# Turning q and k of batch 2 by DMA instead of on the tensor engine, in a fused attention and feed-forward kernel

## The chip, the cores and the metric

The kernel runs on one core of a Trainium2 chip. The core has a tensor engine (PE, with a separate queue of weight loads, PEld), a vector engine (DVE), a scalar engine (ACT), GpSimd (POOL) and a sync engine (SP) that only issues transfers, and 16 DMA engines that serve them all. Each engine runs its own instructions strictly in the order in which the program gives them, and waits on semaphores for the others. The metric is device time in microseconds for one execution. Three runs of the kernel before took 352.36, 352.91 and 353.14 us, median 352.91.

## What is computed

Causal attention with a decay, for 8 batches, 8 heads, 576 positions and a head width of 64; its result, 4608 tokens of 512, goes through `x @ w_in`, `h - tanh(h)` and `@ w_out` with an inner width of 2048.

```python
scores = scale * np.matmul(q, k.transpose(0, 1, 3, 2))
cum = np.cumsum(np.log(np.clip(f, 0.0001, 1.0)), axis=-1)
scores = np.where(causal, -1000000000.0, scores + cum[:, :, :, None] - cum[:, :, None, :])
attn = softmax(scores)                       # over the last axis
x = (attn @ v).transpose(0, 2, 1, 3).reshape(B * S, H * D)
h = x @ w_in
out = (h - np.tanh(h)) @ w_out
```

## The kernel before, in words

The order of the work on all five engines is written out by hand. The outer loop runs over 32 *slots*, one for each pair of heads: slot p works on batch p // 4 and heads 2c and 2c+1 with c = p % 4. A slot has seven *tiles* (ti = 0 to 6), and each tile is one `scores` call: PE multiplies a strip of keys with queries into one of two PSUM banks (`ps_sc`), ACT takes the exponential (L324) into a buffer `e` (`el` for tile 3), and POOL masks the diagonal (L334). Tiles 0 to 2 belong to the first head, 4 to 6 to the second, 3 to both. At tile 2 of the next slot `values` multiplies the masked weights with v on PE (L346, one PSUM tile `av`, a single buffer), and DVE normalises the result (L353 to L355, `rs` and `xn`). `turn` then brings `xn` into a ring `XR` by a DMA transpose from SP (L369, L371).

Between the tiles the feed-forward work is dealt out as *items* of four or eight matmuls: `mlp1` (L397, `hps`, then tanh on ACT, L402, and a sum on DVE, L406) and `mlp2` (L432 for the first 512 tokens, L456 for the rest, which use Strassen's seven products; DVE makes the sums, L424, and the weight differences, L234). `TAKE` says how many items a slot gets: 2, 7, 6, 6, 6, 8, 8, 7, 7 in slots 4 to 12. When the slots are done the rest of the items runs alone. Item banks come from a ring (`RINGS`): three banks `ps_m` up to slot 10, and a fourth, `ps_tr`, from slot 11 (`widen(1)`).

Scores need q and k with the head width on partitions (`QT`, `KT`, each in two buffers by batch parity). There are two ways to that:

* Batches below `FAR` (0, 1 and 2): a whole tensor is loaded with `load_qk` (L90). For each pair, in the slot before it is needed, `trans` turns it by six PE transposes (L253) into PSUM (`ps_tr` from slot 4 on) and two copies bring the even and the odd columns to `QT` or `KT` (L266 on DVE, L264 on ACT). From slot 4 on, q's copies are one on DVE and one on ACT, k's are both on DVE. The turn of k stands at tile 2 ahead of `values`, that of q at tile 0.
* Later batches: `load_block` (L96) loads five blocks of rows from POOL's queue, `turn_block` (L101) turns each by a DMA transpose on SP's queue into `TQ` or `TK`, and `place` copies them to `QT` (L106 on ACT, L108 on DVE or POOL) and `KT`. There is one tile `TQ`.

A dictionary `LOADS`, keyed by (slot, tile), holds when each load, turn and copy is emitted; it comes right behind that tile's scores. POOL's loads use eight completion semaphores in turn, so that a load waits until the load eight before it has landed; that wait stands in POOL's own queue.

Of the kernel before, what the change touches and what calls it, by code (L numbers as in the profile page):

```python
# [17 lines left out]
FAR = 3  # L18
# [3 lines left out]
def kernel(  # L22
# [63 lines left out]
    TQ = qkp.tile([P, NPAIR, S], FP16, tag="TQ", name="TQ")  # L86
# [35 lines left out]
    lf = TQ[0:NH, :, :].rearrange("p c s -> p (c s)").bitcast(FP32)[:, 0:S]  # L122
# [35 lines left out]
    cum = TQ[0:NH, :, :].rearrange("p c s -> p (c s)").bitcast(FP32)[:, S:2 * S]  # L158
# [47 lines left out]
    LOADS.setdefault((NPAIR, 5), []).append(lambda: load_qk(qn, q, 2, 0, H))  # L206
    LOADS.setdefault((NPAIR, 6), []).append(lambda: load_qk(kn, k, 2, 0, H))
    for b in range(2, B):
        p0 = (b - 1) * NPAIR
        for n in range(NJ - 1):  # L210
            LOADS.setdefault((p0 + 1, n), []).append(lambda b=b, n=n: load_v_block(b, n, 0, H))
        LOADS.setdefault((p0 + 1, 4), []).append(lambda b=b: load_v_rest(b))
        LOADS.setdefault((p0, 0), []).append(lambda b=b: load_aug(b))
        if b < FAR:
            continue
        for n in range(NJ):
            qs, ts = ((p0 - 1, n), (p0, 4)) if b == FAR else ((p0 - 2, n + 2), (p0 - 1, 3 if b == FAR + 1 else 1))
            LOADS.setdefault(qs, []).append(lambda b=b, n=n: load_block(qb, q, b, n))
            LOADS.setdefault((p0, n), []).append(lambda b=b, n=n: load_block(kb, k, b, n))
            LOADS.setdefault(ts, []).append(lambda b=b, n=n: turn_block(TQ, qb, b, n))  # L220
            LOADS.setdefault((p0 + 1, 4), []).append(lambda b=b, n=n: turn_block(TK, kb, b, n))
        parts = [(dst, src, a, c) for dst, src in ((QT, TQ), (KT, TK)) for a in range(2) for c in (0, 2)]
        spots = [(p0, 3, "A"), (p0, 5, "A"), (p0 + 1, 0, "A"), (p0 + 1, 2, "A")] + [(p0 + 3, ti, "V") for ti in range(4)]
        if b == FAR:
            spots = [(p0 + 3, ti, eng) for ti, eng in zip((0, 1, 2, 0, 1, 2, 4, 5), "AVAPPPPP")]
        elif b == FAR + 1:
            spots[0:4] = (p0, 5, "A"), (p0, 6, "A"), (p0 + 1, 0, "A"), (p0 + 1, 2, "V")
        for (slot, ti, eng), (dst, src, a, c) in zip(spots, parts):
            LOADS.setdefault((slot, ti), []).append(lambda b=b, dst=dst, src=src, a=a, c=c, eng=eng: place(
                dst, src, b, a, c, eng))  # L230
# [5 lines left out]
    SPOTS = [(7, 1), (7, 2), (7, 4), (7, 5), (8, 1), (8, 2), (10, 6), (11, 0)]  # L236
# [6 lines left out]
    def trans(b, c, src, dst, early, copies, split=False):  # L243
# [25 lines left out]
        for fn in todo[:2]:  # L269
            fn()  # L270
        return todo[2:]

    def head_tiles(a):
        return [[(a, 0, 0, 512, 0)],
                [(a, 1, P, 448, 0), (a, 0, 512, 64, 448)],
                [(a, 2, 2 * P, 320, 0), (a, 3, 3 * P, 192, 320)]]

# [109 lines left out]
    def mlp1(u, ft, part=None):  # L387
        if part != 1:
            HP[(u, ft)] = bank("hps")
        hps = HP[(u, ft)]  # L390
        t0 = u * UW % RING
        parts = [(0, t0, min(UW, RING - t0))]
        if t0 + UW > RING:
            parts.append((RING - t0, 0, t0 + UW - RING))
        for o, t, n in parts:
            for ci in {None: range(NCH), 0: range(NCH - 1), 1: (NCH - 1,)}[part]:
                nc.tensor.matmul(out=hps[:, o:o + n], lhsT=win[:, ci, ft * P:(ft + 1) * P],  # L397
                                 rhs=XR[:, ci, t:t + n], start=(ci == 0), stop=(ci == NCH - 1))
        if part == 0:
            return  # L400
        th = tmp.tile([P, UW], FP32, tag="th", name="th")
        nc.scalar.activation(out=th, in_=hps, func=AF.Tanh, scale=-1.0)  # L402
        half, i, kt = ft // NK, ft % NK // 4, ft % 4
        if half == 0 and kt == 0:
            GQ[(u, i)] = gtp.tile([P, 2, NK // 2, UW], FP16, tag="gq", name="gq")
        nc.vector.tensor_tensor(out=GQ[(u, i)][:, half, kt, :], in0=hps, in1=th, op=ALU.add)  # L406
        if u >= PLAIN:
            at = (12, 13, 14, 15) if u == 1 else (3, 6, 9, 12)
            if ft in at:
                sums(u, "S3", at.index(ft))  # L410
# [100 lines left out]
    def start():  # L511
# [5 lines left out]
        k_rest = trans(*pairs[0], kn, KT, True, "VVVV", True)  # L517
        unread(22)
# [18 lines left out]
    def att_items(p):  # L537
# [7 lines left out]
        early = p < NPAIR  # L545
        for ti in range(len(TILES)):
# [7 lines left out]
            if p == 1 and ti == 3:  # L554
                put(last)
            for load in LOADS.get((p, ti), ()):
                items.append((load, False))
            at_q, at_k = (1, 3) if p == 0 else (0, 1) if early else (0, 2) if p == NPAIR else (0, 2)
            if ti == at_q and after and after[0] < FAR:
                put(trans, *after, qn, QT, early, "VV" if early else "VA")  # L560
# [32 lines left out]
    with tc.manual_schedule(engines=FIVE):  # L593
        bulk()
        for p in range(len(pairs) + 1):
# [3 lines left out]
            if p == 3 * NPAIR - 1:  # L599
# [48 lines left out]
```

## Time and profile before

| | us |
|---|---|
| median of three runs | 352.91 |
| the profiled execution, whole | 352.82 |
| its span, first to last instruction | 351.0 |
| PE busy | 336.5 |
| DVE busy | 259.9 |
| ACT busy | 236.0 |
| POOL busy | 167.6 |

The granted clock of the tensor engine is full in every slice. The start of `values` marks the slots: 31.08 us in slot 4, 44.26 in slot 5, 54.65 in slot 6, 63.05, 71.12, 80.27, 90.83 and 100.48 in slots 7 to 11, 110.17 in slot 12. The profiled execution lies within 0.1 us of the median, and outside the span 1.8 us are left. In a timeline a row gives start, duration, engine, line, operation, tiles, form and count of a run of equal instructions, and in brackets how long the engine had been idle and what ended that. The end of a matmul is modelled and includes the way through the array, so a stall of PE is read from start to start: a 512-column matmul follows the one before after 0.216 us.

### The profile page before, as it was taken

How to read it: one execution, taken by the hardware profiler on the slowest of the kernel's cores; microseconds unless marked ns; L12 is line 12 of the kernel's file. 1: busy time of each engine (PE TensorE's matmuls, PEld its weight loads, DVE VectorE, ACT ScalarE, POOL GpSimd, SP SyncE). 2: the span in 40 equal slices, each digit the busy share in tenths (PEclk: the TensorE clock that was granted, in tenths of full speed). 3: DMA queues.
4: the chain of work that ended last, by engine and by line, in shares of the span. 5: the costliest groups of instructions: out<-in, count | busy, mean ns of one | idle time of the engine just before them, and what ended most of it. 6: DMA issues, size and time to landing. Idle time of an engine off the chain costs nothing.

```text
span 351.0 us, 8590 instructions
## 1 busy us (share of the span) xinstructions
PE 336.5 (96%) x3253; PEld 230.7 (66%) x3253; DVE 259.9 (74%) x493; ACT 236.0 (67%) x433; POOL 167.6 (48%) x324
## 2 busy tenths in 40 slices
PE   8998888999889999999999999999999999999996
PEld 7476444555458655875588888855885587477485
DVE  7597577747799588767876787678767866876874
ACT  5587777668695778588868886888648841742640
POOL 8873563776499656575657564752322210000000
PEclk9999999999999999999999999999999999999999
DMA  9999999999978999699969996992031013003003
GB/s 112 144 166 202 192 206 127 112 150 175 113 62 110 152 169 133 77 172 159 114 78 179 151 111 88 174 157 42 23 102 49 18 36 122 0 2 120 0 6 115
DMA packets 144876, 38.79 MB, mean 111 GB/s; under 512 B 128148, under 2 KB 143236, under 8 KB 144836
## 3 DMA queue, kind: packets, MB, share of 16 engines
q0 software_dynamic: 92480, 18.39, 69.7%
q1 hardware_dynamic: 52356, 19.88, 29.7%
q8 instruction: 25, 0.41, 0.5%
q14 instruction: 15, 0.12, 0.1%
HBM read 36.85 MB, written 9.44 MB: 132 GB/s over the span
## 4 chain that ended last, share of the span: by engine, by line
PE 77%; DVE 11%; ACT 7%; issue 2%; DMA 1%; POOL 1%; ACTq 0%; DVEq 0%; POOLq 0%
PE hps L397 28%; PE ops L456 26%; PE ps L315 10%; PE av L346 6%; PE ops L432 3%; ACT e L324 3%; DVE KT L266 3%; DVE gq L406 2%; ACT th L402 2%; DVE QT L266 2%; DVE xn L355 1%; ACT QT L264 1%; PE t L253 1%; DVE gq L424 1%; DMA TQ<-in_f_dram 1%
## 5 line engine op out<-in xcount | busy, mean ns | idle before, releaser
L397 PE MATMUL hps<-XR,win 128*128 128x512 f16 (+1 forms) x640 | 141.4, 357 | 3.1 <-DVE gq L406 1.6
L406 DVE TENSOR_TENSOR gq<-hps,th 128x512 f16<-128x512 f32 x144 | 98.6, 687 | 33.1 <-ACT th L402 31.8
L324 ACT ACTIVATE e<-ps 128x512 f16<-128x512 f32 x192 | 110.0, 598 | 15.5 <-PE ps L315 7.9
L402 ACT ACTIVATE th<-hps 128x512 f32<-128x512 f32 x144 | 86.8, 604 | 49.5 <-PE hps L397 44.3
L334 POOL TENSOR_SCALAR_AFFINE_SELECT e<-e 128x128 f16<-128x128 f16 x168 | 60.6, 363 | 76.7 <-ACT e L324 74.8
L397 PEld LDWEIGHTS <-win 128*128 128x128 f16 x640 | 57.6, 97 | 50.3 <-issue 2.8
L315 PE MATMUL ps<-QT,KT 67*128 67x64 f16 (+5 forms) x384 | 77.2, 276 | 3.1 <-ACT e L324 2.4
L456 PEld LDWEIGHTS <-gq 128*128 128x128 f16 x640 | 60.3, 97 | 12.3 <-DVE gq L424 1.4
L456 PE MATMUL ops<-wout,gq 128*128 128x256 f16 x512 | 63.3, 272 | 1.1 <-DVE gq L424 1.1
L315 PEld LDWEIGHTS <-KT 67*128 67x128 f16 (+1 forms) x384 | 36.9, 98 | 27.9 <-issue 4.8
L346 PEld LDWEIGHTS <-e 128*128 128x128 f16 x896 | 32.1, 97 | 3.1
L346 PE MATMUL av<-vn,e 128*128 128x65 f16 x896 | 33.6, 193 | 0.0
L119 POOL DMA_DIRECT2D vn<-in_v_dram x32 | 28.0, 877 | 10.6 <-DMA win<-in_moe_w_in_dram 4.1
L456 PE MATMUL ops<-W,sq 128*128 128x256 f16 x256 | 31.2, 272 | 0.0
L355 DVE TENSOR_TENSOR xn<-av,rs 128x640 f16<-128x640 f32 x32 | 26.4, 825 | 1.1
L456 PEld LDWEIGHTS <-sq 128*128 128x128 f16 x256 | 24.2, 98 | 3.4
L266 DVE COPY KT<-t 64x576 f16<-64x576 f16 (+1 forms) x26 | 19.5, 750 | 3.8 <-PE t L253 3.6
L334 POOL TENSOR_SCALAR_AFFINE_SELECT el<-el 128x128 f16<-128x128 f16 x28 | 9.5, 338 | 26.8 <-ACT el L324 26.7
L96 POOL DMA_DIRECT2D qn<-in_q_dram x25 | 21.2, 846 | 0.7 <-issue 0.4
L96 POOL DMA_DIRECT2D kn<-in_k_dram x25 | 21.1, 846 | 0.6 <-issue 0.3
L106 ACT ACTIVATE QT<-TQ 64x1152 f16<-64x1152 f16 x17 | 19.7, 1158 | 0.2
L266 DVE COPY QT<-t 64x576 f16<-64x576 f16 x15 | 11.9, 795 | 7.6 <-PE t L253 7.6
(83 smaller groups left out, 301.9 us busy)
## 6 DMA issues: line engine op xcount, KB each, us to landing
out_dram<-ost SPq DMA_DIRECT2D x34, 256.0 KB
vn<-in_v_dram POOLq DMA_DIRECT2D x24, 128.0 KB, 5.6
qn<-in_q_dram POOLq DMA_DIRECT2D x20, 128.0 KB, 4.9
kn<-in_k_dram POOLq DMA_DIRECT2D x20, 128.0 KB, 4.5
win<-in_moe_w_in_dram POOLq DMA_DIRECT2D x2, 1024.0 KB, 14.8
wout<-in_moe_w_out_dram POOLq DMA_DIRECT2D x2, 1024.0 KB, 14.0
XR<-xn SPq DMA_TRANSPOSE x56
vn<-in_v_dram POOLq DMA_DIRECT2D x12, 64.0 KB, 4.8
```

What stands on the lines that cost most here:

```text
L96: nc.gpsimd.dma_start(out=dst[b % 2][0:pn, n, :].rearrange("p (h d) -> p h d", h=H), in_=src[b, :, n * P:n * P + pn, :].rearrange("h p d - ...
L119: nc.gpsimd.dma_start(out=vn[b % 2][:, n, h0:h1, 0:D], in_=v[b, h0:h1, n * P:(n + 1) * P, :].rearrange("h p d -> p h d"))
L266: nc.vector.tensor_copy(out=to, in_=of)
L315: nc.tensor.matmul(out=ps[:, col:col + n], lhsT=KT[b % 2][0:rows, h, j * P:(j + 1) * P], rhs=QT[b % 2][0:rows, h, i0:i0 + n], start=not ow ...
L324: nc.scalar.activation(out=e[:, lo:hi], in_=ps[:, lo:hi], func=AF.Exp, scale=qscale)
L334: nc.gpsimd.affine_select(out=view, in_=view, compare_op=ALU.is_ge, fill=0.0, base=0, pattern=pat, channel_multiplier=-1)
L346: nc.tensor.matmul(out=av[:, a, ib, :], lhsT=E.pop((b, c, a, j, ib)), rhs=vn[b % 2][:, j, 2 * c + a, 0:D + 1], start=(j == 0), stop=(j == ib))
L355: nc.vector.tensor_tensor(out=xn.rearrange("p i (a d) -> p a i d", a=2), in0=av[:, :, :, 0:D], in1=rs.to_broadcast([P, 2, NJ, D]), op=ALU. ...
L397: nc.tensor.matmul(out=hps[:, o:o + n], lhsT=win[:, ci, ft * P:(ft + 1) * P], rhs=XR[:, ci, t:t + n], start=(ci == 0), stop=(ci == NCH - 1))
L402: nc.scalar.activation(out=th, in_=hps, func=AF.Tanh, scale=-1.0)
L406: nc.vector.tensor_tensor(out=GQ[(u, i)][:, half, kt, :], in0=hps, in1=th, op=ALU.add)
L456: nc.tensor.matmul(out=ps[:, m, :], lhsT=LHS[lhs](u, kt // 4)[:, kt % 4, m * P:(m + 1) * P], rhs=rhs[:, kt, :], start=(fresh and (apart or ...
```

## The change

* `FAR` is 2: batch 2 goes the second way too. Its five blocks of q are loaded from tile 3 of slot 4 to tile 0 of slot 5, those of k in tiles 1 to 5 of slot 5, v in slot 6 instead of slot 5. q is turned on SP at (5, 2), k at (6, 1). ACT places q at (6, 5), (7, 0), (8, 1), (8, 5), DVE places k at (7, 2), (7, 4), (8, 2), (8, 6). The PE transposes of slots 7 to 10 and their copies are gone.
* `TQ` has two tiles, by batch parity.
* Of the remaining turns from slot 4 on (batch 1, slots 4 to 6) both q copies are on DVE, and of q and k the second copy is emitted a tile later (`LATER`, `rest`). In slots 5 and 6 the turn of k moves from tile 2, ahead of `values`, to tile 3, behind it.
* Batch 3: q is placed by ACT alone and k by DVE alone (before: ACT, DVE, ACT and five copies on POOL), in slots 11 and 12. Batch 4: all four q copies on ACT (before: three and one on DVE). For all later batches k's copies are spread over two slots, (p0+3, 0), (p0+3, 2), (p0+4, 1), (p0+4, 4).
* The four-bank ring starts at slot 7 instead of 11.
* The weight differences move to (7,1), (7,3), (7,5), (7,6), (8,0), (8,4), (9,5), (10,1), and the first Strassen sums `S3` of unit 1 come with `mlp1` steps 3, 6, 9, 12, as in the other units, instead of 12 to 15.

```diff
-FAR = 3
+FAR = 2
...
-    TQ = qkp.tile([P, NPAIR, S], FP16, tag="TQ", name="TQ")
+    TQ = [qkp.tile([P, NPAIR, S], FP16, tag=f"TQ{i}", name=f"TQ{i}") for i in range(2)]
...
-    LOADS.setdefault((NPAIR, 5), []).append(lambda: load_qk(qn, q, 2, 0, H))
-    LOADS.setdefault((NPAIR, 6), []).append(lambda: load_qk(kn, k, 2, 0, H))
...
     for b in range(2, B):
         p0 = (b - 1) * NPAIR
...
+        at_q = [(p0 - 2, n + 2) for n in range(NJ)]
+        at_k = [(p0, n) for n in range(NJ)]
+        at_v = [(p0 + 1, n) for n in range(NJ)]
+        to_q, to_k = (p0 - 1, 1), (p0 + 1, 4)
+        on_q = (p0, 3), (p0, 5), (p0 + 1, 0), (p0 + 1, 2)
+        on_k = (p0 + 3, 0), (p0 + 3, 2), (p0 + 4, 1), (p0 + 4, 4)
+        if b == 2:
+            at_q = [(p0, 3), (p0, 4), (p0, 5), (p0, 6), (p0 + 1, 0)]
+            at_k = [(p0 + 1, n + 1) for n in range(NJ)]
+            at_v = [(p0 + 2, n) for n in range(NJ)]
+            to_q, to_k = (p0 + 1, 2), (p0 + 2, 1)
+            on_q = (p0 + 2, 5), (p0 + 3, 0), (p0 + 4, 1), (p0 + 4, 5)
+            on_k = (p0 + 3, 2), (p0 + 3, 4), (p0 + 4, 2), (p0 + 4, 6)
+        elif b == 3:
+            at_q = [(p0 - 1, n) for n in range(NJ)]
+            to_q = p0, 4
+            on_q = (p0 + 3, 1), (p0 + 3, 3), (p0 + 3, 5), (p0 + 4, 1)
+            on_k = (p0 + 3, 2), (p0 + 3, 4), (p0 + 4, 0), (p0 + 4, 4)
...
+            add(to_q, turn_block, TQ[b % 2], qb, b, n)
+            add(to_k, turn_block, TK, kb, b, n)
+        for n, (c, a) in enumerate(((0, 0), (0, 1), (2, 0), (2, 1))):
+            add(on_q[n], place, QT, TQ[b % 2], b, a, c, "A")
+            add(on_k[n], place, KT, TK, b, a, c, "V")
...
-    SPOTS = [(7, 1), (7, 2), (7, 4), (7, 5), (8, 1), (8, 2), (10, 6), (11, 0)]
+    SPOTS = [(7, 1), (7, 3), (7, 5), (7, 6), (8, 0), (8, 4), (9, 5), (10, 1)]
...
-        for fn in todo[:2]:
+        n = 2 if early else 1
+        for fn in todo[:n]:
             fn()
-        return todo[2:]
+        LATER.extend(todo[n:])
+        return todo[n:]
...
+    def rest():
+        while LATER:
+            LATER.pop()()
...
-            at = (12, 13, 14, 15) if u == 1 else (3, 6, 9, 12)
+            at = 3, 6, 9, 12
...
+            if p >= NPAIR and ti in (at_q + 1, at_k + 1) and after and after[0] < FAR:
+                items.append((rest, False))
...
-            at_q, at_k = (1, 3) if p == 0 else (0, 1) if early else (0, 2) if p == NPAIR else (0, 2)
+        at_q, at_k = (1, 3) if p == 0 else (0, 1) if early else (0, 2) if p == NPAIR else (0, 3)
...
-                put(trans, *after, qn, QT, early, "VV" if early else "VA")
+                put(trans, *after, qn, QT, early, "VV")
...
-            if p == 3 * NPAIR - 1:
+            if p == 2 * NPAIR - 1:
                 widen(1)
```

More of the change, by code (lines that the diff above doesn't have):

```diff
@@ L120, in load_v_block @@
                             in_=v[b, h0:h1, n * P:(n + 1) * P, :].rearrange("h p d -> p h d"))
-    lf = TQ[0:NH, :, :].rearrange("p c s -> p (c s)").bitcast(FP32)[:, 0:S]
+    lf = TQ[0][0:NH, :, :].rearrange("p c s -> p (c s)").bitcast(FP32)[:, 0:S]
     nc.sync.dma_start(out=lf, in_=f.rearrange("b h s -> (b h) s"))
@@ L157 @@
     nc.scalar.activation(out=lf, in_=lf, func=AF.Ln)
-    cum = TQ[0:NH, :, :].rearrange("p c s -> p (c s)").bitcast(FP32)[:, S:2 * S]
+    cum = TQ[0][0:NH, :, :].rearrange("p c s -> p (c s)").bitcast(FP32)[:, S:2 * S]
     nc.vector.tensor_tensor_scan(out=cum, data0=ones16, data1=lf, initial=0.0,
@@ L205, with add @@
         LOADS.setdefault((3, n), []).append(lambda n=n: load_v_block(1, n, 2, H))
-    LOADS.setdefault((NPAIR, 5), []).append(lambda: load_qk(qn, q, 2, 0, H))
-    LOADS.setdefault((NPAIR, 6), []).append(lambda: load_qk(kn, k, 2, 0, H))
+    def add(where, fn, *args):
+        LOADS.setdefault(where, []).append(lambda: fn(*args))
     for b in range(2, B):
         p0 = (b - 1) * NPAIR
[L210 to L215, printed above, removed]
-        for n in range(NJ):
[L217 to L230, printed above, removed]
@@ new lines @@
+        add((p0, 0), load_aug, b)
+        for n in range(NJ):
+            add(at_q[n], load_block, qb, q, b, n)
+            add(at_k[n], load_block, kb, k, b, n)
+            if n < NJ - 1:
+                add(at_v[n], load_v_block, b, n, 0, H)
+            else:
+                add(at_v[n], load_v_rest, b)
+            add(to_q, turn_block, TQ[b % 2], qb, b, n)
[3 more added lines that the diff above has]
+            add(on_k[n], place, KT, TK, b, a, c, "V")
@@ L276, in head_tiles @@
                 [(a, 2, 2 * P, 320, 0), (a, 3, 3 * P, 192, 320)]]
+    LATER = []
+    def rest():
+        while LATER:
+            LATER.pop()()
     TILES = head_tiles(0) + [[(0, 4, 512, 64, 64), (1, 4, 512, 64, 128)]] + head_tiles(1)
@@ L517, in start @@
         k_rest = trans(*pairs[0], kn, KT, True, "VVVV", True)
+        LATER.clear()
         unread(22)
```

## The prediction, made before the changed kernel ran

> **What bounds the kernel now.** I read the page's busy times first, then PE's waits by stretch, then PE's timeline where a stall stands, then the other engines' timelines there.
>
> ```profile
> PE 336.5 (96%) x3253; PEld 230.7 (66%) x3253; DVE 259.9 (74%) x493; ACT 236.0 (67%) x433; POOL 167.6 (48%) x324
> ```
>
> PE leads. Its list of waits from 130 to 340 us is empty: from slot 14 on the time is PE's own work in sequence. So the change can win only before 130 us, in two ways: fewer PE instructions, or fewer stalls. PE's timeline:
>
> ```profile
> 41.37 1.03 PE L397 MATMUL hps<-XR,win 128*128 128x512 f16 x4
> 43.15 0.41 PE L253 MATMUL t<-id,kn 96*128 96x96 f16 x6 [0.75 <-ACT QT L264]
> 43.40 1.03 PE L397 MATMUL hps<-XR,win 128*128 128x512 f16 x4
> ...
> 54.40 0.42 PE L253 MATMUL t<-id,kn 96*128 96x96 f16 x6 [0.86 <-ACT QT L264]
> ...
> 88.67 0.38 PE L315 MATMUL ps<-QT,KT 67*128 67x320 f16 x2
> 89.71 0.41 PE L253 MATMUL t<-id,kn 96*128 96x96 f16 x6 [0.66 <-ACT QT L264]
> 89.97 1.03 PE L397 MATMUL hps<-XR,win 128*128 128x512 f16 x4
> ...
> 94.28 1.02 PE L397 MATMUL hps<-XR,win 128*128 128x512 f16 x4 [0.38 <-DVE gq L406]
> ...
> 105.32 0.39 PE L456 MATMUL ops<-wout,gq 128*128 128x256 f16 x2 [1.08 <-DVE gq L424]
> ```
>
> Two things are to be seen. Six transposes take 0.25 to 0.26 us from their start to the next row's (43.15 to 43.40). And a stall is larger than its bracket, because the end of a matmul is modelled late: four matmuls at 41.37 take 0.865, so PE stood from 42.24 to 43.15, 0.91 us. From start to start the stalls are: slots 4 to 6: 0.97 (before 33.38), 0.91, 0.80, 0.31, 1.02; slots 7 to 9: none; slots 10 and 11: 0.82, 0.54, 0.70 (before 96.06), 1.24; slots 12 to 14, all for exponentials of ACT: 0.39, 0.44, 0.53.
>
> **PE work removed.** 8 groups (slots 7 to 10, q and k) x 0.257 = 2.06 us, all on the path.
>
> **Stalls of slots 10 and 11.** The 0.82 is a turn of k waiting for ACT's copy out of the one bank of q's turn; it goes with the turn. The 0.54 and 0.70 wait for DVE to free one of three banks; slots 9 and 10 lose six DVE copies of 0.80 and get a fourth bank. The 1.24 waits for the last S3 sum: DVE runs without a gap from 97.75 to 106.4, and the change takes two weight differences (0.77 each), a q copy (0.65) and most sums out of that stretch. DVE in slot 10 then has 8 x 0.687 + 3 x 0.6 + 0.77 + 1.2 = 9.3 us against 8 items x 0.865 + 2.27 = 9.2 of PE, so it is level, with one bank more. I count 3.30 gone; bounds 2.0 and 3.3.
>
> **Stalls of slots 12 to 14.** Two stand behind three q copies of 1.16 us on ACT, one exponential between them (115.07, 116.62, 118.28); the third behind ACT's tanh waiting 0.87 for a DVE that had a q copy. The change spaces batch 4's copies as those of later batches stand, which stall nothing, but puts three more copies (3.5 us) on ACT in slots 11 to 13. ACT was busy 1.78 of 5 us from 110 to 115 and 2.78 from 120 to 125, so they fit. I take 0.9 of the 1.36; bounds: all gone, or 1.5 more.
>
> **Slots 4 to 6.** ACT's q copy goes to DVE, and with it ACT's wait for DVE's half (1.46 at 42.29); k's turn stands a tile later. Up to 4.0 us of stalls could go. But new waits follow, on transfers that PE's lead doesn't move:
>
> ```profile
> 31.11 0.82 POOL L119 DMA_DIRECT2D vn<-in_v_dram  x1 [4.12 <-DMA win<-in_moe_w_in_dram]
> 32.17 0.88 POOL L193 DMA_DIRECT2D wout<-in_moe_w_out_dram  x1
> 35.09 0.88 POOL L193 DMA_DIRECT2D wout<-in_moe_w_out_dram  x1
> ...
> 49.36 1.30 SPq L369 DMA_TRANSPOSE XR<-xn  x1
> ...
> 77.53 6.54 SPq L101 DMA_TRANSPOSE TQ<-qn  x5
> ...
> 42.29 0.81 ACT L264 ACTIVATE QT<-t 64x576 f16<-64x576 f16 x1 [1.46 <-DVE QT L266]
> ```
>
> (1) *POOL.* The first row shows POOL stopped 4.12 us for the landing of the load eight before. `wout` lands 12.9 and 15.2 us after issue, at 45.1 and 50.3. Ten block loads now follow it at once, and the third block of k, at (5, 3), is the eighth after the second `wout`: POOL stands from about 47 to 50.3. Behind it are the masks of tiles 4 to 6 of slot 5 and two loads of 0.88: 50.3 + 0.88 + 0.3 + 0.88 + 0.3 + 0.7 + 0.42 = 53.8. `values` in slot 6 needs them and ends about 54.3 (before: 55.55). Of 4.0 us only 1.25 are left.
>
> (2) *ACT behind TQ.* Loads of v of this shape landed 0.6 to 1.25 us apart, so q's blocks land from 51.2 to about 54.4. SP needs 1.3 each (6.54 for five): 51.3 to 57.8. Packets come later under bulk loads: the XR turn of 49.36 has none in its queue until 53.0. A quiet one lands about 2 us after issue. I take 60.5 for the last, bounds 59.2 and 63. ACT reaches (6, 5) at about 57.5 and blocks; the copy ends 61.65, the exponential of tile 6 at 62.2, and PE's (7, 1) scores, which need its bank and would start at 54.3 + 4 x 0.865 + 0.26 + 0.93 = 58.95, start at 62.25: a new stall of 3.3 us.
>
> (3) *DVE behind TK.* SP goes on with XR (2.6, to 60.4), then TK (6.5, to 66.9), landing 68.3. DVE's copy at (7, 2) waits for it, with rs, xn and the weight differences behind it; it ends 68.8. PE reaches slot 8 at 62.25 + 5 x 0.865 + 0.90 + 1.16 = 68.64, so it waits 0.15. `values` of slot 8 starts at 68.8 + 2 x 0.865 + 0.66 = 71.2, where before it started at 71.12, with four of the eight groups already gone. The xn of slot 7 comes at 70.0, that of slot 8 at 74.8; XR lands about 79.2 and `mlp1` of unit 1 asks at 80.4, so nothing is lost there.
>
> By start of `values` in slot 8, then, the change has lost 0.1 us, whatever was won in slots 4 to 6.
>
> The Trainium skill ("VectorE: DVE Perf Modes", The three transpose paths) gives 1309 ns for a DMA transpose of 128x128; one after another, the 18 squares of q would be 23.6 us by an estimate from it, TK would land past 98 us and the time would rise by about 27 us. The trace disagrees: five turns are issued in 6.54 us, and batch 3's TK, issued from 87.42, was read at 101.5.
>
> **Edits at nothing.** Two TQ tiles (SP waited 6.1 us for the one, with no PE wait behind it); k copies of later batches spread (0.46 each on a DVE with gaps; price 0 to 0.5); v in slot 6 (needed in slot 9, two slots after landing). Five copies of 1.1 to 1.6 us leave POOL in slot 11, hidden behind PE before.
>
> **Sum.** +0.1 (slots 4 to 8) - 1.03 (four groups of slots 9 and 10) - 3.30 - 0.9 = -5.1, from the profiled 352.8 (0.1 under the median): **347.7 us**.
>
> **The rivals.**
> *A, transfers later than that: slower.* Bulk loads starve SP's queue; every microsecond that TK lands after 68.3 delays slot 8 by as much. It decides from 68.3 + 5.1 = 73.4 us. For it: the turn of 49.36 took until after 57 in all. Against: later turns kept SP's pace beside loads. With TK at 75, 354.4. 0.14.
> *B, no new waits.* If the transfers hide, the front stalls stay away too: at the fastest SP issues, 1.2 each, TK lands near 67.2, which by (3) gives 1.1 more, and all of slots 12 to 14 gives 0.46: 346.1; without gates on transfers 342.7. 0.12.
> *C, ACT becomes the bound in slots 11 to 13.* Three more copies, 3.5 us, with only half hidden, and none of the 1.36 won: 347.7 + 0.9 + 1.8 = 350.4. For it: the stalls there were ACT's already. Against: the same spacing later. 0.12.
> *D, the clock.* A stall of 3.3 us is longer than any in the trace, whose longest is 1.24, and the clock was full throughout. If half the clock were granted for as long again, 3.3 us of work would take 6.6: 351.0. 0.05. The Trainium skill ("TensorE: Matmul & The Clock Gate", Why this matters for your kernels) warns of idle gaps over about 3 us between bursts, after which the clock halves; no run here shows it.
> *E, nothing happens.* What slots 10 and 11 stop losing is lost there to DVE, level with PE in slot 10, and only the groups remain: 347.7 + 3.3 + 0.9 + 0.8 = 352.7. 0.05.
>
> **How the numbers follow.** The forecast holds 0.52. The range takes in B's near end and C and D: 346.0 to 351.5, leaving out the most of A, E and the far end of B, 2 in 10. A change of 0.2%, 0.7 us, is about what can be told from none. Faster: forecast 0.52, B, C and D 0.29 = 0.81. Within 0.2%: 0.05, E. Slower: 0.14, A.
>
> **What would show it.** Right: no L253 after 60 us; the four stalls of slots 10 and 11 gone; a POOL load of k with an idle of some 3 us ended by `wout`; an ACT copy from TQ near 60 us with a wait before it; a PE stall of 2 to 4 us before scores of slot 7; `values` of slot 8 near 71. Wrong: DVE's copy from TK later than 73; PE stalls for exponentials in slots 11 to 13; a clock below full near 62 us.

## The result, and the profile after

The changed kernel takes 356.02 us (median; 355.24 to 357.21), the kernel before 352.55 beside it: a ratio of 1.0098, with an interval of 1.0073 to 1.0123. It is slower by 3.5 us, where 347.7 was forecast. The profiled execution took 355.64 us, so 7.9 us are to be explained.

The page of the changed kernel: its busy times, and the clock in 40 slices of 8.84 us.

```profile
PE 334.3 (95%) x3205; PEld 229.0 (65%) x3205; DVE 252.8 (72%) x490; ACT 239.7 (68%) x433; POOL 168.1 (48%) x327
...
PEclk9999999699999999999999999999999999999999
```

PE has 2.2 us less to do (334.3 for 336.5), and yet the span grew from 351.0 to 353.6. The clock, full throughout before, falls in one slice, from 62 to 71 us. Its list of waits (in total, times, longest):

```profile
PE ps L334 <- ACT e L343: 9.1, 10, 5.4
PE ps L334 <- DVE KT L277: 2.0, 2, 1.1
PE av L365 <- POOL e L353: 1.5, 2, 0.8
```

The waits for `gq` of slots 10 and 11 are gone; one wait of 5.4 us has come. PE's timeline shows where:

```profile
53.11 0.27 PE L365 MATMUL av<-vn,e 128*128 128x65 f16 x3 [0.69 <-POOL e L353]
...
54.16 0.45 PE L365 MATMUL av<-vn,e 128*128 128x65 f16 x9 [0.79 <-POOL e L353]
...
59.30 1.03 PE L451 MATMUL ops<-wout,gq 128*128 128x512 f16 x4
65.75 0.59 PE L334 MATMUL ps<-QT,KT 67*128 67x448 f16 x2 [5.43 <-ACT e L343]
66.15 1.90 PE L451 MATMUL ops<-wout,gq 128*128 128x512 f16 x4
...
73.75 0.60 PE L334 MATMUL ps<-QT,KT 67*128 67x320 f16 x3
...
111.37 0.38 PE L334 MATMUL ps<-QT,KT 67*128 67x448 f16 x2 [1.04 <-ACT e L343]
```

The four matmuls of 59.30 are through at 60.17 (4 x 0.216), so PE stood for 5.6 us. After it the same four take 1.90 instead of 1.03. The third matmul of the row at 73.75 is the first scores of slot 8, at 73.97. The other engines' timelines hold what PE waited for:

```profile
50.72 0.88 POOL L96 DMA_DIRECT2D kn<-in_k_dram  x1 [3.87 <-DMA wout<-in_moe_w_out_dram]
...
51.60 6.66 SPq L101 DMA_TRANSPOSE TQ<-qn  x5
...
60.96 8.10 SPq L101 DMA_TRANSPOSE TK<-kn  x5
...
64.06 1.16 ACT L106 ACTIVATE QT<-TQ 64x1152 f16<-64x1152 f16 x1 [5.77 <-DMA TQ<-qn]
...
72.44 0.63 DVE L108 COPY KT<-TK 64x1152 f16<-64x1152 f16 x1 [12.84 <-DMA TK<-kn]
```

ACT stood 5.77 us for TQ with the exponentials queued behind it, and DVE 12.84 us for TK. DVE's copy of TK was over at 73.07 (72.44 + 0.63), 0.9 us before PE came to the first scores of slot 8, so in this execution PE did not wait for TK there. And the clock, in stretches of 2 us (length; busy time and instructions of PE, PEld, DVE, ACT and POOL; the granted clock; the DMA engines' busy share; GB/s):

```profile
60.00:62.00 2.00, 0.33 (x2) 0.05 (x1) 0.00 (x0) 0.00 (x0) 0.01 (x1) 1.00 2.00 156
62.00:64.00 2.00, 0.00 (x0) 0.00 (x0) 0.00 (x0) 0.00 (x0) 0.00 (x0) 0.70 1.92 159
64.00:66.00 2.00, 0.25 (x1) 0.10 (x1) 0.00 (x0) 1.94 (x3) 0.23 (x1) 0.50 1.78 72
...
68.00:70.00 2.00, 2.00 (x34) 1.77 (x32) 0.00 (x0) 0.60 (x1) 1.81 (x4) 0.60 1.70 227
```

In stretches of 1 us the clock falls to one half at 62.8 and is full again at 69.6.

| start of values in slot | before | after | forecast |
|---|---|---|---|
| 5 | 44.26 | 41.54 | |
| 6 | 54.65 | 51.74 | |
| 7 | 63.05 | 68.27 | |
| 8 | 71.12 | 76.35 | 71.2 |
| 11 | 100.48 | 103.95 | |
| 14 | 129.35 | 131.58 | |
| end of span | 351.0 | 353.6 | |

The front won 2.9 us by slot 6 and lost 8.1 by slot 7. From slot 8 to the end 2.7 came back: 5.23 behind, then 2.53 (the spans are 353.58 and 351.05 before rounding). From the first scores of slot 8 to the end of the span the changed kernel takes 279.6 us.

### The profile page after: what moved, and what is told of

It is laid out like the page before. It is cut to its first block, busy times and chain, and to the rows that moved or that the text cites. A ratio compares the mean times of both kernels' runs of the same rounds, so it can differ in the third digit from the quotient of the medians.

```text
span 353.6 us, 8525 instructions
## 1 busy us (share of the span) xinstructions
PE 334.3 (95%) x3205; PEld 229.0 (65%) x3205; DVE 252.8 (72%) x490; ACT 239.7 (68%) x433; POOL 168.1 (48%) x327
## 4 chain that ended last, share of the span: by engine, by line
PE 83%; ACT 4%; DMA 3%; issue 3%; DVE 3%; SPq 1%; POOL 1%; ACTq 0%; POOLq 0%
PE hps L416 30%; PE ops L475 26%; PE ps L334 12%; PE av L365 8%; PE ops L451 3%; ACT e L343 3%; DMA TQ<-qn 2%; DMA kn<-in_k_dram 1%; DVE gq L425 1%; SPq L101 1%; PE ps L337 1%; PE t L264 1%; ACT th L421 1%; PE ps L305 1%; PE idle L524 1%
## 5 line engine op out<-in xcount | busy, mean ns | idle before, releaser
L353 POOL TENSOR_SCALAR_AFFINE_SELECT e<-e 128x128 f16<-128x128 f16 x168 | 60.4, 362 | 72.3 <-ACT e L343 70.2
L334 PE MATMUL ps<-QT,KT 67*128 67x64 f16 (+5 forms) x384 | 78.1, 278 | 11.3 <-ACT e L343 9.1
L475 PEld LDWEIGHTS <-gq 128*128 128x128 f16 x640 | 60.3, 97 | 11.0
L365 PEld LDWEIGHTS <-e 128*128 128x128 f16 x896 | 33.0, 98 | 5.3 <-POOL e L353 1.7
L365 PE MATMUL av<-vn,e 128*128 128x65 f16 x896 | 34.6, 194 | 1.5 <-POOL e L353 1.5
L106 ACT ACTIVATE QT<-TQ 64x1152 f16<-64x1152 f16 x24 | 27.9, 1163 | 6.3 <-DMA TQ<-qn 5.8
L96 POOL DMA_DIRECT2D kn<-in_k_dram x30 | 25.3, 845 | 6.3 <-DMA wout<-in_moe_w_out_dram 5.7
L96 POOL DMA_DIRECT2D qn<-in_q_dram x30 | 25.4, 846 | 3.0 <-issue 2.0
L108 DVE COPY KT<-TK 64x1152 f16<-64x1152 f16 x24 | 11.5, 481 | 13.2 <-DMA TK<-kn 12.8
L372 DVE TENSOR_SCALAR rs<-av 128x10 f32<-128x10 f32 x32 | 5.2, 162 | 21.8 <-PE av L365 21.7
```

Source lines behind the costliest of these rows:

```text
L96: nc.gpsimd.dma_start(out=dst[b % 2][0:pn, n, :].rearrange("p (h d) -> p h d", h=H), in_=src[b, :, n * P:n * P + pn, :].rearrange("h p d - ...
L106: nc.scalar.activation(out=to, in_=of, func=AF.Copy)
L334: nc.tensor.matmul(out=ps[:, col:col + n], lhsT=KT[b % 2][0:rows, h, j * P:(j + 1) * P], rhs=QT[b % 2][0:rows, h, i0:i0 + n], start=not ow ...
L353: nc.gpsimd.affine_select(out=view, in_=view, compare_op=ALU.is_ge, fill=0.0, base=0, pattern=pat, channel_multiplier=-1)
L365: nc.tensor.matmul(out=av[:, a, ib, :], lhsT=E.pop((b, c, a, j, ib)), rhs=vn[b % 2][:, j, 2 * c + a, 0:D + 1], start=(j == 0), stop=(j == ib))
L475: nc.tensor.matmul(out=ps[:, m, :], lhsT=LHS[lhs](u, kt // 4)[:, kt % 4, m * P:(m + 1) * P], rhs=rhs[:, kt, :], start=(fresh and (apart or ...
```

## The experiments

Each ratio is to the kernel before, run beside it (352.46 to 352.54 us median), with its interval. The theory after the result: batch 2's turned q and k arrive too late, TK above all, and slot 8 can't start before TK. The rivals: ACT's queue alone holds PE up, the clock costs on top, or other parts of the change cost it. "Too late" holds in what follows; "TK above all" does not: in which runs PE did wait for TK is said with each.

**q copied later** (e1_q_late).

```diff
-            on_q = (p0 + 2, 5), (p0 + 3, 0), (p0 + 4, 1), (p0 + 4, 5)
+            on_q = (p0 + 3, 4), (p0 + 3, 6), (p0 + 4, 1), (p0 + 4, 5)
```

> ACT's first two copies of batch 2's q move from (6, 5), (7, 0) to (7, 4), (7, 6), the last places that still lie before the scores of slot 8. Nothing else is changed. Theory 'transfers' (the landing of TK at 72.4 us sets the start of slot 8, whatever PE does before): the stall of 5.4 us before scores (7, 1) goes, but PE then reaches the scores of slot 8 near 66 us and waits there for DVE's copy of TK, to 73.1 us or later; values of slot 8 starts between 75 and 77, the time is 354.5 to 357. Rival 'ACT's queue' (the wait of ACT at (6, 5) alone holds PE up): the stall of 5.4 us and the slow clock of 3.3 us behind it go, no new stall comes: 347 to 348.5.

359.01 us, 1.0186 (1.0170 to 1.0201). The stall before (7, 1) is gone, and a larger one stands before the first scores of slot 8, in PE's timeline:

```profile
66.19 0.38 PE L334 MATMUL ps<-QT,KT 67*128 67x320 f16 x2
75.64 0.61 PE L334 MATMUL ps<-QT,KT 67*128 67x512 f16 x1 [9.06 <-DVE KT L108]
76.04 1.91 PE L451 MATMUL ops<-wout,gq 128*128 128x512 f16 x4
```

ACT's queue alone is not the cause: without its wait PE only came sooner to TK, and now it did wait for it. The time is worse than either theory had it, because TK was read at 75.13 us in this execution and the half clock (to 79.7) now fell wholly on work of slot 8.

**PE kept busy in the stall** (e2_warm).

```diff
+            if p == 7 and ti == 1:
+                items.append((lambda: unread(95), False))
```

> 95 matmuls of 128 columns on constants, into a bank that nobody reads, are put ahead of the scores (7, 1), where PE stands idle from 60.2 to 65.7 us. All waits stay. If an idle PE is what halves the clock, the clock stays full from 62 to 70 us. Theory 'the clock is hidden' (what PE loses at half clock it would have lost waiting for TK): scores (8, 0) move from 74.1 to about 73.2 us, 354.6 to 355.5. Rival 'the clock adds to the stall': 3.3 us less, 352.2 to 353.2. If the clock drops all the same, something else drops it, and the time stays at 356.

355.0 us, 1.0061 (1.0043 to 1.0079). PE's timeline and the stretch of the clock in this run:

```profile
70.71 0.39 PE L334 MATMUL ps<-QT,KT 67*128 67x512 f16 x1 [0.43 <-DVE KT L108]
```

```profile
64.00:66.00 2.00, 2.00 (x39) 1.48 (x38) 0.00 (x0) 1.91 (x3) 1.46 (x4) 1.00 1.26 145
```

An idle PE is what halved the clock: with matmuls in the gap it stays full. And PE now waits for TK at slot 8. In the changed kernel PE came to those scores 0.9 us after the copy of TK had ended; that is what the clock could cost there. The difference of the two ratios is 1.3 us, uncertain by 1.1 (both intervals together), so a cost of 0.9 fits. The 3.3 us of the rival were also my mis-sizing: from 65.75 to 69.6 at half clock 1.9 us are lost, and times alone don't tell 1.9 from 0.9; the wait for TK in the trace does.

**Without the loads of v of batch 2** (e3_no_v2).

```diff
-            if n < NJ - 1:
+            if b == 2:
+                pass
+            elif n < NJ - 1:
                 add(at_v[n], load_v_block, b, n, 0, H)
```

> The five loads of v of batch 2 in slot 6 are left out (batch 2 then works with batch 0's v, and its rows of the output are those of another v). The turns of q and k on SP's queue run beside these loads from 54 to 68 us. Theory 'the turns share the DMA engines with the loads of v': TQ lands near 61.5 instead of 64.0, TK near 69 instead of 72.4, the stall before (7, 1) shrinks to about 3 us and the time falls to 351 to 353.5. Rival 'the turns are slow by themselves': TQ at 63.5 to 64, TK at 72, the time within 0.7 us of 356.

353.1 us, 1.0013 (0.9993 to 1.0032). TQ came as early as expected, TK only in part:

```profile
60.45 1.16 ACT L106 ACTIVATE QT<-TQ 64x1152 f16<-64x1152 f16 x1 [3.13 <-DMA TQ<-qn]
```

```profile
70.22 0.56 DVE L108 COPY KT<-TK 64x1152 f16<-64x1152 f16 x1 [11.60 <-DMA TK<-kn]
```

So the loads of v do delay the turn of q, at a price of some 3 us of time. PE came to slot 8 at 71.31, 0.5 us after the copy of TK had ended.

**The same bytes in an eighth of the packets** (e13_wide).

```diff
+    def load_wide(dst, src, b, n):
+        pn = min(P, S - n * P)
+        nc.gpsimd.dma_start(out=dst[b % 2][0:pn, n, :],
+            in_=src[b, :, :, :].rearrange("h (p r) d -> (h p) (r d)", r=8)[n * P:n * P + pn, :])
```

> As the changed kernel, but the ten block loads of batch 2's q and k read the same number of bytes as rows of 1024 B that lie together in memory, instead of eight pieces of 128 B for each position. The contents are then those of other positions, so batch 2's scores are not the reference's; every transfer, turn and copy still takes place, with 128 packets to a full block instead of 1024. Theory 'the number of small packets fills the DMA engines' (a packet of 128 B takes 32 ns, one of 1 KB 98 ns, so a block falls from about 2.0 to 0.8 us of all 16 engines): k's last block lands 6 us or more earlier than 60.2, TQ before 60, TK at 66 to 69; the time is 348 to 352. Rival 'the turns themselves are what is slow': TQ and TK land within 1.5 us of 64 and 72.4, the time is 354.5 to 357.

354.4 us, 1.0047 (1.0030 to 1.0063): between the two. TQ was read at 62.30 and TK at 69.98. PE came to slot 8 only at 73.43, 3.0 us after the copy of TK had ended: after its stall for TQ the clock was at one half until 70.39.

**Both at once** (e15_wide_no_v2).

> As e13_wide (q and k of batch 2 read as 1 KB rows, so with contents of other positions), and the five loads of v of batch 2 are left out as in e3_no_v2: nearly all 128 B packets beside the turns of TQ and TK are gone. Theory 'the turns get the DMA engines only in the gaps of POOL's queue': TQ lands at 59 to 60.5 and TK at 66.5 to 68.5, as the forecast had them, the stall before (7, 1) is 2 to 3.3 us, and the time is 349 to 351.5. Rival 'the turns are slow by themselves': TQ no earlier than 61.5, TK no earlier than 69.5, the time 352.5 or more.

355.0 us, 1.0076 (1.0048 to 1.0104): TQ as the theory had it, TK and the time as the rival. SP, ACT and DVE in this run:

```profile
49.67 6.58 SPq L106 DMA_TRANSPOSE TQ<-qn  x5
...
58.93 7.11 SPq L106 DMA_TRANSPOSE TK<-kn  x5
...
57.89 1.16 ACT L111 ACTIVATE QT<-TQ 64x1152 f16<-64x1152 f16 x1 [1.67 <-DMA TQ<-qn]
...
70.08 0.45 DVE L113 COPY KT<-TK 64x1152 f16<-64x1152 f16 x1 [12.19 <-DMA TK<-kn]
```

TQ was readable 1.6 us after its last turn was issued, sooner than the forecast had it; TK was not. TK's last turn was issued at 66.04, and it was read 4.0 us later. Beside it now run the loads of batch 3's q, which stand in slot 7 and come earlier when nothing holds POOL up: their five blocks were issued from 60.3 to 66.3 here, from 66.5 to 73.9 in the changed kernel. PE then stood 4.46 us for TK, the clock halved again, and the whole was no faster. From 66 to 68 us, counted in the trace, SP's queue moved 415 packets and POOL's 1677. So what was taken out of the DMA queue was filled from behind. That these loads are what held TK up fits also the run with q copied later, where they were issued from 60.4 us on and TK was later still; no run takes them away. The landings side by side, in the profiled execution of each run:

| run | last turn of q issued by | TQ read | last turn of k issued by | TK read | PE begins slot 8 |
|---|---|---|---|---|---|
| the changed kernel | 58.25 | 64.06 | 69.06 | 72.44 | 73.97 |
| PE kept busy | 55.53 | 61.64 | 66.00 | 70.20 | 70.71 |
| without v | 57.07 | 60.45 | 66.83 | 70.22 | 71.31 |
| wide packets | 57.41 | 62.30 | 67.26 | 69.98 | 73.43 |
| both | 56.25 | 57.89 | 66.04 | 70.08 | 70.59 |

The times of one kernel scatter by 2 us (355.24 to 357.21 for the changed one), so a single row carries little; "PE kept busy" is the changed kernel up to its idle gap, and yet its turns of q were issued 2.7 us sooner. But TK was read before 69.9 in none of them. From the last issue to the reading, which leaves this scatter out, TQ took 5.8, 6.1, 3.4, 4.9 and 1.6 us: it follows what stands beside it. TK took 3.4, 4.2, 3.4, 2.7 and 4.0.

The last column is what sets the time: from it to the end of the span are 279.6 us in the first four rows, and 281.9 in the last, where the half clock lies behind it. PE waited for TK there in the second and the last row; in the other three it came 0.9, 0.5 and 3.0 us after the copy of TK had ended, held up by TQ and then by the half clock.

**q's loads ahead of wout** (e12_q_first).

```diff
-             (4, 0): [lambda: load_wout(0, NFT // 2)],
-             (4, 2): [lambda: load_wout(NFT // 2, NFT)]}
+             (4, 2): [lambda: load_wout(0, NFT // 2)],
+             (4, 4): [lambda: load_wout(NFT // 2, NFT)]}
...
+            at_q = [(p0 - 1, 4), (p0 - 1, 5), (p0 - 1, 6), (p0, 0), (p0, 1)]
+            at_k = [(p0, 5), (p0, 6), (p0 + 1, 0), (p0 + 1, 1), (p0 + 1, 2)]
+            to_q, to_k = (p0, 6), (p0 + 2, 0)
```

> As the changed kernel, but the blocks of batch 2's q are loaded ahead of wout (from (3, 4) to (4, 1), wout at (4, 2) and (4, 4)), k's from (4, 5) to (5, 2); q is turned from (4, 6) on, k at (6, 0). All transfers are the same ones, only their order differs. Theory 'the order of the transfers decides': TQ lands before 57 us, so ACT does not wait at (6, 5); SP turns k right behind XR or before it, TK lands at 66 to 69; wout lands at 50 to 56, before or about when mlp2 asks for it at 56; the time is 347.5 to 352.5. Rival 'the DMA engines have no room for batch 2's blocks before 68 us in any order': wout or v late instead, a stall of 3 us or more in slots 5 to 8, 354 or more.

357.97 us, 1.0161 (1.0135 to 1.0186): the rival. SP's rows, then DVE's and PE's:

```profile
40.47 11.04 SPq L101 DMA_TRANSPOSE TQ<-qn  x5
...
58.69 8.53 SPq L101 DMA_TRANSPOSE TK<-kn  x5
```

```profile
73.47 0.45 DVE L108 COPY KT<-TK 64x1152 f16<-64x1152 f16 x1 [15.55 <-DMA TK<-kn]
```

```profile
73.98 0.61 PE L334 MATMUL ps<-QT,KT 67*128 67x512 f16 x1 [6.60 <-DVE KT L108]
```

With q in place 11 us earlier, its turns took 11.04 us to issue instead of 6.66, and TQ was read at 58.70, while `wout` passed. k's blocks, now all behind `wout`, landed from 58.7 to 63.6. Counted in the trace, packets of the two queues in stretches of 2 us:

| from | POOL's queue | SP's queue |
|---|---|---|
| 48 us | 313 | 308 |
| 50 us | 306 | 304 |
| 52 us | 333 | 338 |
| 54 us | 592 | 597 |
| 56 us | 827 | 821 |

In these ten microseconds they alternate one to one, so the turns went at the pace of the packets beside them: 150 in a microsecond beside packets of 1 KB, 410 beside packets of 128 B, and in the run with both taken out 1571 in 2 us (56 to 58) with nothing beside them. The Trainium skill ("DMA: Bandwidth & Descriptors", Queues, rings and completion order) says that each DMA engine goes round between the queues that have work, a packet at a time; these counts agree. It is not the whole account: in the changed kernel, with turns of q issued and not yet moved, SP's queue moved 208 packets beside 1282 of POOL's from 56 to 58 us, and 467 beside 1584 from 60 to 62. Why it got less than one for one there, no run shows.

**The masks' wait taken away** (e6_k_loads). The last three loads of k move from (5, 3), (5, 4), (5, 5) to (5, 6), (6, 0), (6, 1).

> As the changed kernel, but the last three block loads of batch 2's k are issued at (5, 6), (6, 0), (6, 1) instead of (5, 3), (5, 4), (5, 5), so that POOL does not stand in slot 5 with the masks behind it while the second half of wout lands. Theory 'TK decides': values of slot 6 no longer waits for masks and ends about 1.3 us earlier (53.1 instead of 54.5), the stall before scores (7, 1) grows by as much, since TQ lands no earlier, and the time is 355 to 357.5. Rival 'each wait counts for itself': 1.3 us less, 354.3 to 354.9.

355.56 us, 1.0091 (1.0058 to 1.0124). PE no longer waits for masks in slot 6, and its stall before (7, 1) is 8.57 us instead of 5.43. PE's row and DVE's:

```profile
67.15 0.58 PE L334 MATMUL ps<-QT,KT 67*128 67x448 f16 x2 [8.57 <-ACT e L343]
```

```profile
69.81 0.90 DVE L108 COPY KT<-TK 64x1152 f16<-64x1152 f16 x1 [11.96 <-DMA TK<-kn]
```

The stall grew by 3.1 us, not by the 1.3 of the theory, as TQ was read only at 65.46. PE came to slot 8 at 75.66, 5.0 us after the copy of TK had ended. So the wait for the masks was worth nothing, but because of TQ and the half clock behind it, not of TK. The interval does not shut out the rival's 354.9; the trace, of the slowest of the four executions (357.34 us), speaks against the rival.

**The front as before** (e11_front_old).

```diff
-        n = 2 if early else 1
+        n = 2
...
-                put(trans, *after, qn, QT, early, "VV")
+                put(trans, *after, qn, QT, early, "VV" if early else "VA")
```

(and k's turn at tile 2 in slots 5 and 6.)

> As the changed kernel, but the remaining turns on PE (slots 4 to 6) stand as before: q's copies on DVE and ACT, k's turn at tile 2 ahead of values, both copies at once. Only the front's gain (slots 5 and 6 were 2.7 to 2.9 us ahead of the kernel before) is taken away. Theory 'TK decides': slot 8 starts when TK has landed, whatever the front won, so the time stays at 355 to 357.5. Rival 'the gain of the front still counts': 358 to 359.5.

355.59 us, 1.0063 (1.0029 to 1.0098). Values of slot 6 starts at 54.61 instead of 51.74, and the time is no longer for it. PE's row and DVE's:

```profile
65.00 0.58 PE L334 MATMUL ps<-QT,KT 67*128 67x448 f16 x2 [4.63 <-ACT e L343]
```

```profile
71.20 0.45 DVE L108 COPY KT<-TK 64x1152 f16<-64x1152 f16 x1 [9.45 <-DMA TK<-kn]
```

What PE won in the front was worth nothing, because the transfers decided: here TQ, read at 63.31, with the half clock until 70.69. PE came to slot 8 at 74.10, 2.4 us after the copy of TK had ended.

**Batch 2 on PE, the rest of the change kept** (e4_pe_rest).

```diff
-FAR = 2
+FAR = 3
```

(with batch 2's loads as before, and the four-bank ring from slot 11.)

> Batch 2 is turned on PE again, as in the kernel before (its loads too, and the four-bank ring from slot 11, since the turns need the bank until slot 10); all other parts of the change stay: both copies of a turn on DVE, the second a tile later, the weight differences and sums in their new places, the copies of batches 3 and 4. Theory 'only batch 2's transfers lose': the front keeps its gain (values of slot 6 near 52.5), slots 7 to 10 cost their eight groups of transposes again, slots 11 to 14 gain 1.5 to 2.5 us: 347.5 to 350.5. Rival 'other parts lose too' (DVE with two copies of a turn becomes the bound in slots 7 to 10, or ACT in slots 11 to 13): 352 to 355.

351.75 us, 0.9983 (0.9974 to 0.9993): between the theories. The changed kernel takes 4.3 us more: that is what batch 2's way by DMA costs, with the removed transposes and the earlier fourth bank counted in. The rest of the change gains only 0.6. PE's timeline says why:

```profile
47.96 0.39 PE L340 MATMUL ps<-QT,KT 67*128 67x512 f16 x1 [1.15 <-DVE KT L283]
...
57.34 0.39 PE L340 MATMUL ps<-QT,KT 67*128 67x512 f16 x1 [1.20 <-DVE KT L283]
...
84.92 0.39 PE L340 MATMUL ps<-QT,KT 67*128 67x512 f16 x1 [1.33 <-DVE KT L283]
...
96.74 0.39 PE L340 MATMUL ps<-QT,KT 67*128 67x512 f16 x1 [1.31 <-DVE KT L283]
```

k's turn stands behind values, its second copy a tile later, and by then DVE has `rs`, `xn` and the sums of `mlp1` ahead of it: the next slot's first scores wait.

**k ahead of values again** (e5_k_ahead). As the last, with `at_k` at tile 2.

> As e4_pe_rest (batch 2 on PE, all else of the change), but the turn of k stands at tile 2 ahead of values again, and its second copy at tile 3. In e4_pe_rest PE waited for DVE's second copy of k (put at tile 4) before the first scores of the next slot four times, 1.15 to 1.33 us each. Theory 'the turn of k a tile later does it': these four waits go, and with them 3.5 to 5 us: 347 to 348.5. Rival 'DVE has too much in these slots wherever the copy stands': the waits go elsewhere (to the items' banks or to values), 350.5 to 352.

352.87 us, 1.0001 (0.9988 to 1.0014): the rival, with a median above its 352. Three of the ten executions took 351.3; in the other seven the clock was halved for a while (see the last section). The waits only moved, to the turn of k, which waits for q's second copy:

```profile
42.72 0.43 PE L270 MATMUL t<-id,kn 96*128 96x96 f16 x6 [1.31 <-DVE QT L283]
...
53.16 0.43 PE L270 MATMUL t<-id,kn 96*128 96x96 f16 x6 [1.13 <-DVE QT L283]
...
89.97 0.43 PE L270 MATMUL t<-id,kn 96*128 96x96 f16 x6 [2.25 <-DVE QT L283]
```

**k behind values, one copy on ACT, both at once** (e9_k_act).

```diff
-                put(trans, *after, kn, KT, early, "VV")
+                put(trans, *after, kn, KT, early, "VV" if early else "AV", False, True)
...
-        n = 2 if early else 1
+        n = 2 if early or both else 1
```

> As e4_pe_rest (batch 2 on PE, k's turn at tile 3 behind values), but k's two copies follow the turn at once, the even half on ACT, the odd half on DVE; q's stay on DVE with the second a tile later. Theory 'the second copy of k behind a full DVE is what e4_pe_rest and the front of the changed kernel lose': the four waits before the first scores of slots 6, 7, 10 and 11 go, about 1.4 us each: 346 to 348. Rival 'ACT has no room for it' (tanh and exponentials of the slots with mlp1): waits for exponentials or for ACT's copy instead, 349.5 to 352.

347.50 us, 0.9856 (0.9839 to 0.9872), as the theory had it: 4.25 us less than with batch 2 on PE and both copies of k on DVE. Two things changed at once, the engine of one copy and that the second copy no longer comes a tile later; no run parts them. In the next kernels, which turn k in the same way, no wait of PE for KT is left.

**Fewer copies on ACT in slot 11** (e8_act_spread, e10_k_act_pool). First, batch 3's last two q copies moved from (11, 5), (12, 1) to (13, 4), (13, 6), on the kernel with k ahead:

> As e5_k_ahead, but ACT's copies of batch 3's q for slot 14 move from (11, 5), (12, 1) to (13, 4), (13, 6). In the changed kernel and in e4_pe_rest PE waits 1.04 us for an exponential of slot 11, behind ACT's copy of (11, 5). Theory 'three more copies on ACT cost that stall': 0.6 to 1.1 us less than e5_k_ahead. Rival 'ACT is level with PE there, and the copies only move the stall': within 0.4 us of e5_k_ahead.

353.15 us, 1.0009 (0.9990 to 1.0029): no gain. The executions without a half clock took 351.8, against 351.3 with k ahead. The stall of slot 11 is gone, and one of 1.05 us stands at 125.50, behind the copies of slot 13. Then, on the kernel with k's copy on ACT, the copy of (11, 5) given to POOL:

> As e9_k_act, but ACT's third copy of batch 3's q at (11, 5) is given to POOL (before the change, five of batch 3's eight copies were POOL's). The stall of 1.04 us in slot 11 stands behind this copy in ACT's queue. If that copy is its cause: 0.6 to 1.1 us less than e9_k_act. If ACT is late there anyway: within 0.3 us of it.

346.18 us, 0.9818 (0.9804 to 0.9833), 1.3 less, somewhat more than the 0.6 to 1.1 expected. So this copy was the stall's cause; giving it to POOL paid, moving two copies along ACT did not.

**Sums and weight differences in their old places** (e14_sums_old).

```diff
-            at = 3, 6, 9, 12
+            at = (12, 13, 14, 15) if u == 1 else (3, 6, 9, 12)
...
-    SPOTS = [(7, 1), (7, 3), (7, 5), (7, 6), (8, 0), (8, 4), (9, 5), (10, 1)]
+    SPOTS = [(7, 1), (7, 2), (7, 4), (7, 5), (8, 1), (8, 2), (10, 6), (11, 0)]
```

> As e10_k_act_pool, but the weight differences stand at (7, 1), (7, 2), (7, 4), (7, 5), (8, 1), (8, 2), (10, 6), (11, 0) again and the first Strassen sums of unit 1 come with steps 12 to 15. Theory 'DVE, full in slot 10, held mlp2 up for the last S3 sum': the stall of 1.24 us before the first mlp2 of slot 11 is back, 0.8 to 1.5 us more than e10_k_act_pool. Rival 'the other edits had relieved DVE already': within 0.4 us of it, or less, since DVE then has fewer sums in slot 9.

345.15 us, 0.9793 (0.9776 to 0.9809): 1.0 less, and the stall of 1.24 us does not come back. With the sums in their new places PE still had waited for DVE in slot 9, as the run before shows:

```profile
89.90 0.38 PE L422 MATMUL hps<-XR,win 128*128 128x512 f16 x1 [0.60 <-DVE gq L431]
```

This kernel beats both: 7.4 us under the one before, without turning batch 2 by DMA. Of its waits on PE these are the longest that are left:

```profile
PE ps L340 <- ACT e L349: 2.2, 7, 0.5
PE idle L530 <- DVE warm L127: 1.1, 1, 1.1
PE hps L422 <- ACT XR L392: 1.0, 1, 1.0
```

**Half of batch 2 by DMA** (e7_half). Heads 4 to 7 alone, wanted from slot 10 on.

```diff
+        nc.sync.dma_start_transpose(out=dst[:, 2:4, n * P:n * P + pn], in_=half_view(src, b)[0:pn, n, :])
...
+            to_q, to_k = (p0 + 3, 4), (p0 + 4, 1)
+            on_q = (p0 + 4, 5), (p0 + 5, 1)
+            on_k = (p0 + 5, 0), (p0 + 5, 2)
```

> Only heads 4 to 7 of batch 2 (needed from slot 10 on) are turned by DMA; heads 0 to 3 (slots 8 and 9) go by PE as in the kernel before. Block loads are half as wide, are issued from (5, 5) to (7, 0), turned at (7, 4) and (8, 1), and copied at (8, 5), (9, 1) and (9, 0), (9, 2). The turn of k stands at tile 2 ahead of values, the four-bank ring starts at slot 9, v is loaded in slot 5 as before; all else as in the changed kernel. Theory 'the change lost because slot 8 needed the transfers by 68 us': with a deadline near 86 us no engine waits for TQ or TK, no clock below full, four groups of transposes (1.03 us) less than in e5_k_ahead and its DVE relieved in slots 9 and 10: 345.5 to 348. Rival 'turning by DMA delays other transfers (XR, v) wherever it stands': PE stalls for XR or v in slots 8 to 10, 350 to 355.

356.46 us, 1.0126 (1.0087 to 1.0164): the rival. SP's and PE's rows:

```profile
76.89 6.37 SPq L120 DMA_TRANSPOSE TK<-kn  x5
83.34 1.22 SPq L406 DMA_TRANSPOSE XR<-xn  x1
```

```profile
78.52 0.38 PE L352 MATMUL ps<-QT,KT 67*128 67x448 f16 x2 [2.04 <-ACT e L361]
...
86.56 0.38 PE L434 MATMUL hps<-XR,win 128*128 128x512 f16 x1 [4.15 <-DMA XR<-xn]
```

ACT still came to TQ too early, and the XR turn that `mlp1` needs stood behind TK's five turns on SP. Five turns of half the width take 6.37 us of SP, as five whole ones do (6.5): to halve the heads halved nothing there. A placement that clears SP for XR was not tried.

## Why the prediction was wrong

The step that failed is the landing of the turns, (2) for TQ and (3) for TK. The way from the last issue to the landing was taken as 2.7 and 1.4 us, from quieter stretches, and was 5.8 and 3.4.

The direction is that of rival A, transfers later than that, which was given 0.14, but it did not come by A's path. A was to decide from a TK at 73.4 us; TK was read at 72.44, and PE did not wait for it. TQ held PE up, then the half clock of rival D, and half of C joined them.

* **PE work removed, stalls of slots 10 and 11: right.** No turn after 60 us, and no wait for `gq` is left. But of the reason for the 1.24, that sums and weight differences leave that stretch, the last experiment on the sums leaves little: in a kernel where other copies had left DVE and POOL, moving them cost 1.0.
* **Slots 4 to 6, step 1, POOL: right.** The idle of 3.87 us ended by `wout` is there, and values of slot 6 ended at 54.47 (forecast 54.3). It did not matter.
* **Step 2, "I take 60.5 for the last, bounds 59.2 and 63": the step that failed on PE's own path.** q's blocks landed as forecast (51.55 to 54.70) and the turns were issued as forecast (51.60 to 58.25). The landing was wrong: 64.06, 5.8 us after the last issue, not 2.7. ACT's block and the new stall at (7, 1) were at the places named, 5.6 us instead of 3.3, and the scores of (7, 1) started at 65.75 instead of 62.25, 3.5 us late.
* **The clock.** Rival D came with it. PE's gap of 5.6 us halved the clock for 6.8 us; from 65.75 to 69.6 PE worked at one half and lost 1.9 us, all of it on PE's way to slot 8. Without that loss PE would have waited for TK, so 0.9 us is what a full clock alone could have saved.
* **Step 3, "TK (6.5, to 66.9), landing 68.3": failed too.** TK was issued over 8.10 us, to 69.06, and read at 72.44. From the last issue to the copy it took 2.7 to 4.2 us in the five executions of the table, against the 1.4 taken from a quiet stretch. I had the counter-evidence in the same paragraph, XR's turn of 49.36 without a packet until 53.3, and used it for TQ alone. In the changed kernel TK stood 0.9 us behind what PE lost by TQ and the clock. It is the second gate: with q's copies later, with PE kept busy, with wide packets and no v at once, and with q loaded first, PE did wait for TK.
* **After slot 8.** From 71.2 on the forecast took 5.2 us back; 2.7 came. At values of slot 8 PE had issued 100 matmuls of the items, 104 before: 0.87 of debt that a comparison of slot starts doesn't show. The stall at 111.37 (slot 11) cost about 1.0; that is rival C, behind the ACT copy of 109.68. Another of 0.42 stands at 83.13, and slots 15 to 30 lose 0.4 more to exponentials behind the copies in their new places, where nothing was priced on ACT.

The sum: at slot 8 3.5 (TQ) + 1.9 (clock) - 0.2 (a wait for TK that was forecast there and did not come) = 5.2; 2.5 after it; and 0.3 outside the span (2.1 us instead of 1.8). Together 8.0, for 7.9 measured. An estimate from the same rows: for no change PE would have had to begin slot 8 near 70.9 (352.55 - 279.6 - 2.1), which takes TQ and TK both sooner, and neither alone would have done it. In the profiled execution with PE kept busy it began at 70.71, and that one took 352.41 us.

"Edits at nothing" failed as well. k's turn a tile later had been counted among what removes stalls; in the kernel with batch 2 on PE it made four, and it took the copy on ACT, emitted at once, to be rid of them.

## What to carry to other kernels

The landing of a transfer is no constant behind its issue: it is to be priced by what stands in the other queues at that time, and by what moves up when that is taken away. When work is moved from a full engine to another resource, ask first when the result is wanted and whether that resource has free time before then; here PE gave up 2.1 us of work and got 5.6 us of waiting. Where two results come late, find out which one holds the engine in each run: with the wait for TQ gone, TK held PE up, and nothing was won. A late copy is best given to an engine that has room at that moment: one copy of each k turn on ACT, emitted at once, was worth 4.25 us, twice what all removed transposes were.

## What the runs showed of the hardware

*The clock gate near 2.4 us.* In the kernel with k ahead of values PE stands from 87.56 to 89.97. Three of its ten times are 351.26 to 351.28, seven 352.61 to 352.91; the mean clock is 0.998 or 0.999 in the three and 0.993 to 0.995 in the seven. The kernel with the spread copies has the same stall; its profiled execution was one with the lower clock, while that of the kernel with k ahead was one of the three. First the kernel with the spread copies, then the one with k ahead, in the same stretch:

```profile
90.00:92.00 2.00, 2.00 (x10) 0.97 (x11) 1.30 (x2) 0.00 (x0) 0.00 (x0) 0.53 1.07 112
```

```profile
90.00:92.00 2.00, 2.00 (x40) 1.52 (x41) 1.34 (x3) 0.60 (x1) 0.00 (x0) 1.00 1.10 112
```

The same gap of 2.4 us halved the clock in one and not in the other, at 1.6 us of time. In the changed kernel the clock fell 2.6 us after the last matmul and returned 3.9 after the next; with q's copies later, 3.1 and 4.1. In the ten traces in which it fell to one half at such a gap, it stayed there for 3.41, 6.83 or 10.24 us: one, two or three times the same length. With the spread copies it fell at 90.12, so the 3.41 us before held the whole gap, and about 1 us of work. The Trainium skill ("TensorE: Matmul & The Clock Gate", What's actually happening) puts it down to windows of about 3.4 us that run freely, and its section Why this matters for your kernels warns of gaps over about 3 us. These lengths, and that the same gap only sometimes counts, agree with a free-running window; that 2.4 us are enough does not agree with a whole idle window of 3.4, and the measurement decides here.

*Small turns cost SP as much as large ones*: 6.37 us for five of half the width, 6.5 for five whole ones.
